# Sliding-window attention and a gated MLP on one core: queries permuted in blocks, the order restored in the output transposes

## The chip, the cores and the metric

The kernel runs on one core of a Trainium2 chip. The core has five engines with queues of their own: TensorE (PE, matmuls, with its weight loads shown as PEld), VectorE (DVE), ScalarE (ACT), GpSimd (POOL) and SyncE (SP). DMA is started from the queues of SyncE, ScalarE and GpSimd. The metric is the device time of one execution in microseconds, the median of several runs. A profile is one further execution, in which every instruction is recorded.

## The reference

Attention has 8 batches, 8 heads, 576 tokens and a head dimension of 64; all inputs are float32. Each query sees itself and the 127 tokens before it, and a bias grows with the distance, with another slope for each head. The result of all heads, 4608 tokens by 512, goes through an MLP with 2048 hidden units.

```
scores = scale * np.matmul(q, k.transpose(0, 1, 3, 2))
rel = pos[:, None] - pos[None, :]
mask = (rel >= 0) & (rel < window)
scores = np.where(mask, scores + bias[None], -1000000000.0)
attn = np.exp(scores - np.max(scores, axis=-1, keepdims=True))
attn = attn / (np.sum(attn, axis=-1, keepdims=True) + 1e-09)
attn_out = np.matmul(attn, v)
x = attn_out.transpose(0, 2, 1, 3).reshape(B * S, H * D)
h = x @ w_in
out = (h * (1.0 / (1.0 + np.exp(-beta * h)))) @ w_out
```

## The kernel before

**Attention of batches 0 and 1** works by pairs of heads, p = 0 to 3, on the first 512 tokens. get_pair loads q or k of a pair with four tokens in a row to each partition, so that a partition reads 1 KB at once; partition r holds tokens 4r to 4r+3. get loads v with the tokens of a block of 128 in the order c, r (token 4r+c on partition 32c+r), in four DMAs of 64 KB, one for each c. cast_pair and cast_v turn these to bf16 on GpSimd. TP transposes q and k on TensorE, and VectorE copies them into QK: k in blocks of 128 tokens, each in the order c, r, and q in the order c, r over all 512 tokens. SP_ computes scores with keys on the partitions. The first matmul puts the bias and the mask from a table into PSUM, the others add k times q. To get queries in their natural order, SP_ reads q with a stride: 128 elements lie between neighbours. A visit "A" covers three pieces (384 columns a head), "B" the other four (512 columns). "A" writes the PSUM tile SS and "B" the tile SX, two banks each. ScalarE's exp makes pt. PVP multiplies with v, and norm divides by the sum, which is a column of ones in VS. XP transposes the result by four matmuls with an identity and VectorE copies it into XT. The last 64 tokens of both batches are a tail: TT, SCT, PV and X, with the tables tablet.

**Batches 2 to 7** load whole blocks, transpose q and k by DMA (DT), and compute scores with SC, without tables: exp with a bias for each partition, and a multiplication by masks on VectorE.

**The MLP** works on groups g of 512 tokens. Hm or HS computes one of 16 hidden blocks, j, by four matmuls of 512 columns into a bank of psum_h, of which there are two; ScalarE's tanh and a VectorE operation write gT. OS multiplies with W2 into the tile ops. load_w1 and load_w2 are DMAs from GpSimd's queue that cast to bf16.

**Order.** TensorE, SyncE and GpSimd run in the written order throughout; ScalarE and VectorE do so in the first block (L574 to L626), and after it their order is a planner's. The first block is batch 0. On SyncE it issues p0, p1, p2, p3, v2, v3 (q and k of a pair, blocks of v) and beta; v0 and v1 are issued by ScalarE after constants. Then come batch 1's loads, and the first of them waits until w1[1] has landed:

```
g = get_pair("q", 1, 0)
after(g, w1[1])
```

On GpSimd, constants_late and the masks of batches 2 and up (constants_masks) precede the casts of batch 1. A DMA's issue can wait for an earlier DMA to land, and for the buffer of the fst pool (13 of them) to come free. The list second (L661) interleaves batch 1's attention with H of group 0, and spread places the steps of batches 2 and up (att) between the matmuls of the later groups: from item 22 of 40 on for group 1.

Of the kernel before, what the change touches and what calls it, by code (L numbers as in the profile page):

```python
# [19 lines left out]
def kernel(  # L20
# [39 lines left out]
    qtok = const.tile([P, P], F32, name="qtok")  # L60
    pen = const.tile([P, P], F32, name="pen")
    rel = const.tile([P, 3, P], F32, name="rel")
    relt = const.tile([P, 64], F32, name="relt")
    zeros = const.tile([P, 512], BF16, name="zeros")
    table = const.tile([P, H, 3, P], BF16, name="table")
    tablet = const.tile([P, 2, 2, NP, 64], BF16, name="tablet")
# [36 lines left out]

    def constants():
        nc.vector.memset(zeros[:], 0.0)
        nc.vector.memset(warm[:], 0.0)
        nc.scalar.activation(out=warm[:], in_=warm[:], func=ACTF.Exp)
        for _ in range(8):  # L110
            nc.tensor.matmul(
                SS[:, 0, :], lhsT=zeros[:, 0:P], rhs=zeros[:], start=True, stop=True,
                skip_group_check=True)
        for c in range(4):
            nc.gpsimd.iota(
                ktok[32 * c : 32 * c + 32], pattern=[[0, 1]], base=c, channel_multiplier=4,
                allow_small_or_imprecise_dtypes=True,
            )
        nc.gpsimd.iota(
            qtok[:], pattern=[[1, P]], base=0, channel_multiplier=0,  # L120
            allow_small_or_imprecise_dtypes=True,
        )
        make_identity(nc, ident[:])
        nc.vector.tensor_scalar(
            out=qtok[:], in0=qtok[:], scalar1=ktok[:, 0:1], scalar2=None, op0=ALU.subtract)
        for a, cmp in ((0, ALU.is_lt), (1, ALU.is_ge)):
            nc.vector.tensor_scalar(
                out=pen[:], in0=qtok[:], scalar1=0.0, scalar2=FAR, op0=cmp, op1=ALU.mult)
            nc.vector.scalar_tensor_tensor(
                out=rel[:, a], in0=qtok[:], scalar=float(P * a), in1=pen[:], op0=ALU.add,  # L130
                op1=ALU.add)
        nc.vector.tensor_copy(out=rel[:, 2], in_=rel[:, 0])
        for h in range(H):
            nc.vector.tensor_scalar_mul(table[:, h], rel[:], -slopes[h] / qscale)
        for i in range(2):
            nc.vector.memset(VS[i][:, :, :, D : D + 1], 1.0)

    def constants_late():
        nc.gpsimd.iota(
            relt[:], pattern=[[1, 64]], base=0, channel_multiplier=-1,  # L140
            allow_small_or_imprecise_dtypes=True,
        )
        nc.gpsimd.affine_select(
            out=relt[:], in_=relt[:], pattern=[[1, 64]], base=0, channel_multiplier=-1,
            compare_op=ALU.is_ge, fill=FAR,
        )
# [116 lines left out]
    def TP(b, p):  # L263
        src = staged.pop((b, "p", p))
        tps = psum_t.tile([P, 2, 4, P], BF16, name="tps", tag="t")
        for i in range(2):
            for c in range(4):
                nc.tensor.transpose(out=tps[:, i, c], in_=src[:, i, c], identity=ident[:])
        qk = QK[b % 2]
        nc.vector.tensor_copy(  # L270
            out=qk[:, 0, p, 0:FULL], in_=tps[:, 0].rearrange("d c r -> d (c r)"))
        nc.vector.tensor_copy(
            out=qk[:, 1, p, 0:FULL].rearrange("d (n c r) -> d c n r", n=4, c=4),
            in_=tps[:, 1].rearrange("d c (n r) -> d c n r", n=4))

    def TT(b):

# [14 lines left out]

    def SP_(b, vis, p):
        qk = QK[b % 2]
        sps = SS if vis == "A" else SX
        w = WIDTH[vis]
        for e in range(2):
            t = table[:, 2 * p + e]
# [8 lines left out]
        for kb, at, q0, n in VISIT[vis]:  # L307
            for e in range(2):
                if vis == "B" and n == 256:
                    o = sps[:, e, 0:P]  # L310
                    o = bass.AP(tensor=o.tensor, offset=o.offset,
                                ap=[list(o.ap[0]), [384, 2], [1, P]])
                else:
                    o = sps[:, e, at : at + n]
                nc.tensor.matmul(  # L315
                    o, lhsT=qk[64 * e : 64 * e + 64, 1, p, P * kb : P * kb + P],
                    rhs=qk[64 * e : 64 * e + 64, 0, p, 0:FULL].rearrange(
                        "d (c r) -> d r c", c=4)[:, q0 // 4 : (q0 + n) // 4, :],
                    start=False, stop=True, skip_group_check=True,
                )  # L320
        pt = pt_pool.tile([P, 2, 512], BF16, name="pt", tag="pt")
# [147 lines left out]
    def Hm(g, j, cs):  # L469
# [1 line left out]
            gts[g] = gt_pool.tile([P, NFF, TOKG], BF16, name="gT", tag="gT")  # L471
        c0 = (g * TOKG) % XTR
        if cs[0] == 0:
            hs[g, j] = psum_h.tile([P, TOKG], F32, name="hps", tag="hps")
        hps = hs[g, j]
        for c in cs:
            nc.tensor.matmul(  # L477
# [95 lines left out]
    with tc.manual_schedule(engines={ENG.PE, ENG.SP, ENG.Pool}):  # L573
        with tc.manual_schedule(engines={ENG.Activation, ENG.DVE}):  # L574
            for w in ("p0", "p1", "v0", "v1", "p2", "p3", "v2", "v3"):
                n = int(w[1])
                if w[0] == "p":
                    get_pair("q", 0, n)
                    get_pair("k", 0, n)
                elif n >= 2:  # L580
                    get("v", 0, n)
            nc.sync.dma_start(out=bflat[:], in_=moe_beta.rearrange("(j p) -> j p", p=P))
            constants()
            for n in range(2):
                get("v", 0, n, nc.scalar)
            w1 = []
            cast_pair(0, 0)
            TP(0, 0)
# [90 lines left out]
        opening.close()  # L679
        late["o"] = ctx.enter_context(  # L680
            tc.tile_pool(name="psum_o", bufs=2, space=bass.MemoryType.PSUM))
        work = tail(1)
        b2 = jobs(2)
        after_w2 = [True]
# [85 lines left out]
```

## Time and profile before

| | us |
|---|---|
| runs, median of 5 | 366.49 |
| lowest, highest | 364.74, 367.74 |
| profiled execution, its time | 363.82 |
| its span in the trace | 362.1 |
| PE busy | 336.3 |
| ACT busy | 206.8 |
| DVE busy | 199.4 |
| POOL busy | 107.5 |

A time in the profile is counted from the span's start. In the page, a row of digits gives the busy share of each fortieth of the span (9.05 us) in tenths; PEclk is the clock that was granted to TensorE. In a timeline, the columns are start, duration, engine, line, operation, output and inputs, count, and in brackets the engine's idle time before, with what ended it. "SPq" and "ACTq" are issues of DMA by SyncE and ScalarE. In groups, the columns after the shapes are total busy time, mean ns of one, and idle time before them. A table of windows gives, for each stretch, PE's busy time, the granted clock, the DMA share and GB/s.

### The profile page before, as it was taken

The page shows a single profiled execution, that of the slowest core. Times are in us where ns is not written, and L with a number is a line of the kernel's source. Part 1 is how long each engine was busy: PE and PEld are TensorE (multiplying, and loading weights), DVE is VectorE, ACT ScalarE, POOL GpSimd, SP SyncE. Part 2 cuts the span into 40 slices and gives each one's busy share as a digit, 9 for nine tenths or more (in the row PEclk, how much of TensorE's full clock was granted, in tenths as well). Part 3 has the DMA queues.
Part 4 walks back from the last instruction along what each step waited for, and adds up shares of the span by engine and source line. Part 5 has one row for each costly group of instructions (what it writes and reads, how often), then busy time and mean ns, then how long its engine had stood idle before and what let it go on. Part 6 is the DMA issues. An engine that isn't in the chain of part 4 may idle for free.

```text
span 362.1 us, 6353 instructions
## 1 busy us (share of the span) xinstructions
PE 336.3 (93%) x2365; PEld 155.6 (43%) x2365; DVE 199.4 (55%) x447; ACT 206.8 (57%) x392; POOL 107.5 (30%) x206
## 2 busy tenths in 40 slices
PE   7496899799799999989999999999999999999994
PEld 2133334344245444444444444444454445444441
DVE  6036557554367578456738764875487546624500
ACT  1242465454777589458746776676677755426511
POOL 4299733403634342333132414131200010010010
PEclk9589999999899999999999999999999999999999
DMA  7599999993999999891929792971100010020021
GB/s 237 111 141 252 208 174 202 216 179 87 241 207 240 241 196 232 186 230 50 208 90 191 153 217 90 189 164 55 60 1 31 31 58 29 3 87 2 29 86 61
DMA packets 136512, 49.45 MB, mean 137 GB/s; under 512 B 125840, under 2 KB 134048, under 8 KB 136480
## 3 DMA queue, kind: packets, MB, share of 16 engines
q1 hardware_dynamic: 127360, 35.41, 51.0%
q0 software_dynamic: 6944, 13.11, 14.4%
q10 hardware_dynamic: 2176, 0.52, 0.7%
q8 instruction: 18, 0.29, 0.4%
q14 instruction: 14, 0.11, 0.1%
HBM read 36.71 MB, written 9.44 MB: 127 GB/s over the span
## 4 chain that ended last, share of the span: by engine, by line
PE 80%; DVE 8%; ACT 6%; DMA 3%; issue 2%; SPq 1%; ACTq 0%
PE ops L500 33%; PE hps L477 30%; ACT pt L415 4%; PE SS L405 4%; DVE gT L485 3%; DVE pt L419 2%; DMA fst<-in_k_dram 2%; PE pv L444 2%; PE SX L315 2%; PE pv L440 2%; PE xt L455 2%; PE SS L315 1%; ACT sig L484 1%; PE pv L345 1%; PE SX L304 1%
## 5 line engine op out<-in xcount | busy, mean ns | idle before, releaser
L477 PE MATMUL hps<-XT,W 128*128 128x512 bf16 x576 | 145.0, 380 | 5.4 <-DVE gT L485 3.9
L500 PE MATMUL ops<-W,gT 128*128 128x512 bf16 x576 | 142.4, 381 | 0.0
L484 ACT ACTIVATE sig<-hps,beta_h 128x512 bf16<-128x512 f32 x144 | 98.7, 691 | 70.9 <-PE hps L477 65.4
L485 DVE SCALAR_TENSOR_TENSOR gT<-sig,hps 128x512 bf16<-128x512 bf16 x144 | 97.7, 684 | 69.9 <-ACT sig L484 69.3
L415 ACT ACTIVATE pt<-SS,bias 128x256 bf16<-128x256 f32 (+1 forms) x192 | 75.2, 478 | 14.5 <-PE SS L405 14.5
L477 PEld LDWEIGHTS <-W 128*128 128x128 bf16 x576 | 51.8, 98 | 63.3 <-issue 12.7
L500 PEld LDWEIGHTS <-gT 128*128 128x128 bf16 x576 | 52.1, 98 | 56.6 <-issue 1.8
L513 POOL DMA_DIRECT2D out_dram<-osb x34 | 18.5, 543 | 193.3 <-ACT osb L506 193.1
L419 DVE TENSOR_TENSOR pt<-pt,mask 128x1024 bf16<-128x1024 bf16 x48 | 36.4, 758 | 16.5 <-ACT pt L415 16.3
L506 ACT ACTIVATE osb<-ops 128x512 f32<-128x512 f32 x36 | 21.8, 605 | 39.1 <-PE ops L500 39.1
L245 POOL CAST vs<-fst 128x512 bf16<-128x512 f32 (+1 forms) x40 | 24.3, 623 | 26.6 <-DMA fst<-in_v_dram 25.2
L329 DVE RECIPROCAL zs<-pv 128x4 f32<-128x4 f32 (+1 forms) x80 | 13.9, 176 | 31.3 <-PE pv L444 18.1
L330 DVE TENSOR_TENSOR xn<-pv,zs 128x256 bf16<-128x256 f32 (+1 forms) x64 | 26.9, 421 | 1.7
L232 POOL CAST bst<-fst 128x512 bf16<-128x512 f32 (+1 forms) x32 | 19.8, 620 | 12.9 <-DMA fst<-in_q_dram 8.3
L405 PE MATMUL SS<-qkT 64*128 64x256 bf16 (+2 forms) x240 | 19.2, 254 | 2.8 <-ACT pt L415 2.6
L233 POOL CAST bst<-fst 128x512 bf16<-128x512 f32 (+1 forms) x32 | 20.0, 624 | 4.9 <-DMA fst<-in_k_dram 4.8
L444 PE MATMUL pv<-vs,pt 128*128 128x65 bf16 x240 | 20.6, 193 | 0.0
L461 DVE COPY XT<-xt 128x512 bf16<-128x512 bf16 (+1 forms) x32 | 12.3, 385 | 14.1 <-PE xt L455 13.8
L444 PEld LDWEIGHTS <-pt 128*128 128x128 bf16 x240 | 16.1, 97 | 6.7
L405 PEld LDWEIGHTS <-qkT 64*128 64x128 bf16 x240 | 8.2, 94 | 22.3 <-issue 21.6
L440 PE MATMUL pv<-vs,pt 128*128 128x65 bf16 x192 | 17.4, 193 | 0.0
L322 ACT ACTIVATE pt<-SS 128x768 bf16<-128x768 f32 x8 | 6.5, 811 | 18.4 <-DMA fst<-in_v_dram 12.4
(72 smaller groups left out, 171.0 us busy)
## 6 DMA issues: line engine op xcount, KB each, us to landing
out_dram<-osb POOLq DMA_DIRECT2D x34, 256.0 KB, 2.9
fst<-in_q_dram SPq DMA_DIRECT2D x32, 256.0 KB, 5.2
fst<-in_k_dram SPq DMA_DIRECT2D x32, 256.0 KB, 5.1
fst<-in_v_dram SPq DMA_DIRECT2D x24, 256.0 KB, 3.8
W<-in_moe_w_in_dram POOLq DMA_DIRECT2D x4, 512.0 KB, 7.3
W<-in_moe_w_out_dram POOLq DMA_DIRECT2D x4, 512.0 KB, 8.7
fst<-in_v_dram SPq DMA_DIRECT2D x24, 64.0 KB, 4.5
fst<-in_q_dram SPq DMA_DIRECT2D x8, 128.0 KB, 3.7
```

The source lines that it names most:

```text
L245: return nc.gpsimd.tensor_copy(out=VS[b % 2][0:rows, sb, :, 0:D], in_=fs.pop(("v", b, sb))[0:rows])
L330: nc.vector.tensor_tensor(out=xn, in0=pv[0:nq, :, 0:D], in1=zs[0:nq].broadcast_to([nq, 4, D]), op=ALU.mult)
L405: nc.tensor.matmul(o, lhsT=qk[64 * e : 64 * e + 64, 1, p, P * kb : P * kb + P], rhs=qk[64 * e : 64 * e + 64, 0, p, P * kb : P * kb + nq], ...
L415: nc.scalar.activation(out=pt[:, e, cols], in_=sps[:, e, cols], func=ACTF.Exp, scale=qscale, bias=bias[:, half, h : h + 1],)
L419: nc.vector.tensor_tensor(out=pt[:], in0=pt[:], in1=masks[m][:], op=ALU.mult)
L440: nc.tensor.matmul(pv[:, hl, 0 : D + 1], lhsT=weights(b, qb - 1, h, 1), rhs=vs[:, qb - 1, h, 0 : D + 1], start=True, stop=False,)
L444: nc.tensor.matmul(pv[:, hl, 0 : D + 1], lhsT=weights(b, qb, h, 0), rhs=vs[:, qb, h, 0 : D + 1], start=qb == 0, stop=True,)
L477: nc.tensor.matmul(hps[:], lhsT=W1[:, c, bass.ts(j, P)], rhs=XT[:, c, c0 : c0 + TOKG], start=(c == 0), stop=(c == NDM - 1),)
L484: nc.scalar.activation(out=sig[:], in_=hps[:], func=ACTF.Tanh, scale=beta_h[:, j : j + 1])
L485: nc.vector.scalar_tensor_tensor(out=gts[g][:, j, :], in0=sig[:], scalar=1.0, in1=hps[:], op0=ALU.add, op1=ALU.mult)
L500: nc.tensor.matmul(ops_, lhsT=gT[:, j, i * P : i * P + P], rhs=W2[:, j, :], start=(j == 0), stop=(j == NFF - 1),)
L506: nc.scalar.mul(osb[:], ops_, 0.5)
```

## The change

1. Queries of batches 0 and 1 are stored as keys are, in blocks of 128 tokens, each in the order c, r (TP). SP_ reads q without a stride, and queries of scores are in the order c, r. The constant qtok, from which the bias table is made, is counted in that order.
2. XP restores the order. Its four transposes with an identity become four matmuls with a permutation matrix, perm, that constants makes from an iota (nat) and an is_equal on VectorE. The PSUM tile is float32, since these aren't transposes.
3. The tail's second table has the keys in the order c, r and the queries in natural order. It was a copy of a part of table; now constants_late makes it by four iotas and four selects on 32 partitions each, and its multiplications cover both tables at once.
4. All of v of batch 0 is issued by SyncE, in the order p0, p1, v0, v1, p2, p3, v2, v3.
5. load_w1(0) is issued after cast_pair(0, 3), and constants_masks after the last cast of batches 0 and 1. betas comes before constants_late.
6. SX is used in batch 0 alone; batch 1's "B" uses SS too. SX's two banks then go to the pool of ops, and H of group 0 uses them for j = 1, 3, 5, 7, so that it has four banks up to j = 7. Three H blocks, not two, start before XP(0, 3), and the list second is spread over one j fewer.
7. The steps of batch 2 begin at item 17 of group 1, not 22.

```diff
-    relt = const.tile([P, 64], F32, name="relt")
+    relt = const.tile([P, 2, 64], F32, name="relt")
+    nat = const.tile([P, P], F32, name="nat")
+    perm = const.tile([P, P], BF16, name="perm")
...
         nc.gpsimd.iota(
-            qtok[:], pattern=[[1, P]], base=0, channel_multiplier=0,
+            qtok[:].rearrange("p (c r) -> p c r", c=4), pattern=[[1, 4], [4, 32]], base=0, channel_multiplier=0,
...
+        nc.gpsimd.iota(
+            nat[:], pattern=[[1, P]], base=0, channel_multiplier=0,
...
+        nc.vector.tensor_scalar(
+            out=perm[:], in0=nat[:], scalar1=ktok[:, 0:1], scalar2=None, op0=ALU.is_equal)
...
-        nc.gpsimd.tensor_copy(
-            out=tablet[:, :, 1], in_=table[:, :, 1, 0:64].rearrange("k (p e) t -> k e p t", e=2))
+        for c in range(4):
+            rows = slice(32 * c, 32 * c + 32)
+            nc.gpsimd.iota(
+                relt[rows, 1], pattern=[[1, 64]], base=P - c, channel_multiplier=-4,
...
+            nc.gpsimd.affine_select(
+                out=relt[rows, 1], in_=relt[rows, 1], pattern=[[-1, 64]], base=c - 1,
...
         for h in range(H):
             nc.gpsimd.tensor_scalar_mul(
-                tablet[:, h % 2, 0, h // 2], relt[:], -slopes[h] / qscale)
+                tablet[:, h % 2, :, h // 2], relt[:], -slopes[h] / qscale)
...
-        nc.vector.tensor_copy(
-            out=qk[:, 0, p, 0:FULL], in_=tps[:, 0].rearrange("d c r -> d (c r)"))
-        nc.vector.tensor_copy(
-            out=qk[:, 1, p, 0:FULL].rearrange("d (n c r) -> d c n r", n=4, c=4),
-            in_=tps[:, 1].rearrange("d c (n r) -> d c n r", n=4))
+        for i in range(2):
+            nc.vector.tensor_copy(
+                out=qk[:, i, p, 0:FULL].rearrange("d (n c r) -> d c n r", n=4, c=4),
+                in_=tps[:, i].rearrange("d c (n r) -> d c n r", n=4))
...
-        sps = SS if vis == "A" else SX
+        sps = SX if vis == "B" and b == 0 else SS
...
-                    rhs=qk[64 * e : 64 * e + 64, 0, p, 0:FULL].rearrange(
-                        "d (c r) -> d r c", c=4)[:, q0 // 4 : (q0 + n) // 4, :],
+                    rhs=qk[64 * e : 64 * e + 64, 0, p, q0 : q0 + n],
...
-        xt = psum_t.tile([P, 4, P], BF16, name="xt", tag="t")
+        xt = psum_t.tile([P, 4, P], F32, name="xtp", tag="t")
         for n in range(4):
-            nc.tensor.transpose(out=xt[:, n, :], in_=xn[:, n, :], identity=ident[:])
+            nc.tensor.matmul(xt[:, n, :], lhsT=xn[:, n, :], rhs=perm[:], start=True, stop=True)
...
-            hs[g, j] = psum_h.tile([P, TOKG], F32, name="hps", tag="hps")
+            if g == 0 and j < 8 and j % 2:
+                hs[g, j] = late["o"].tile([P, DM], F32, name="hpx", tag="ops")
+            else:
+                hs[g, j] = psum_h.tile([P, TOKG], F32, name="hps", tag="hps")
...
-                elif n >= 2:
+                else:
                     get("v", 0, n)
...
-            for n in range(2):
-                get("v", 0, n, nc.scalar)
...
-            w1.append(load_w1(0))
             TP(0, 2)
...
             cast_pair(0, 3)
+            w1.append(load_w1(0))
...
+            betas()
             constants_late()
-            betas()
-            for j in range(2):
+            opening.close()
+            late["o"] = ctx.enter_context(
+                tc.tile_pool(name="psum_o", bufs=2, space=bass.MemoryType.PSUM))
+            for j in range(3):
                 Hm(0, j, range(3))
             XP(0, 3)
-            for j in range(2):
+            for j in range(3):
                 Hm(0, j, range(3, 4))
...
-        constants_masks()
         cast_pair(1, 0)
...
             cast_v(b, 4)
+        constants_masks()
...
-        for j in range(2, NFF):
+        for j in range(3, NFF):
             HS(0, j)
-            to = len(second) * max(0, j + 1 - 4) // (NFF - 4)
+            to = len(second) * max(0, j + 1 - 5) // (NFF - 5)
...
-        spread([wrap(it, n) for n, it in enumerate(items)], 22, len(items) - 2, need[2])
+        spread([wrap(it, n) for n, it in enumerate(items)], 17, len(items) - 2, need[2])
```

More of the change, by code (lines that the diff above doesn't have):

```diff
@@ L123, in constants @@
         make_identity(nc, ident[:])
+        nc.gpsimd.iota(
+            nat[:], pattern=[[1, P]], base=0, channel_multiplier=0,
+            allow_small_or_imprecise_dtypes=True,
+        )
         nc.vector.tensor_scalar(
@@ L136, in constants @@
             nc.vector.memset(VS[i][:, :, :, D : D + 1], 1.0)
+        nc.vector.tensor_scalar(
+            out=perm[:], in0=nat[:], scalar1=ktok[:, 0:1], scalar2=None, op0=ALU.is_equal)
     def constants_late():
         nc.gpsimd.iota(
-            relt[:], pattern=[[1, 64]], base=0, channel_multiplier=-1,
+            relt[:, 0], pattern=[[1, 64]], base=0, channel_multiplier=-1,
             allow_small_or_imprecise_dtypes=True,
@@ L143, in constants_late @@
         nc.gpsimd.affine_select(
-            out=relt[:], in_=relt[:], pattern=[[1, 64]], base=0, channel_multiplier=-1,
+            out=relt[:, 0], in_=relt[:, 0], pattern=[[1, 64]], base=0, channel_multiplier=-1,
             compare_op=ALU.is_ge, fill=FAR,
         )
-        nc.gpsimd.tensor_copy(
-            out=tablet[:, :, 1], in_=table[:, :, 1, 0:64].rearrange("k (p e) t -> k e p t", e=2))
+        for c in range(4):
+            rows = slice(32 * c, 32 * c + 32)
+            nc.gpsimd.iota(
+                relt[rows, 1], pattern=[[1, 64]], base=P - c, channel_multiplier=-4,
+                allow_small_or_imprecise_dtypes=True,
+            )
+            nc.gpsimd.affine_select(
+                out=relt[rows, 1], in_=relt[rows, 1], pattern=[[-1, 64]], base=c - 1,
+                channel_multiplier=4, compare_op=ALU.is_ge, fill=FAR,
+            )
         for h in range(H):
             nc.gpsimd.tensor_scalar_mul(
-                tablet[:, h % 2, 0, h // 2], relt[:], -slopes[h] / qscale)
+                tablet[:, h % 2, :, h // 2], relt[:], -slopes[h] / qscale)
         for i in range(2):
@@ L676 @@
                 done += 1
-        opening.close()
-        late["o"] = ctx.enter_context(
-            tc.tile_pool(name="psum_o", bufs=2, space=bass.MemoryType.PSUM))
         work = tail(1)
```

## The prediction

> **What bounds the kernel now.** I read the page's row of slices first. TensorE is at nine tenths or more nearly everywhere, except in the first quarter; DMA is full from slice 3 to slice 9.
>
> ```profile
> PE   7496899799799999989999999999999999999994
> PEclk9589999999899999999999999999999999999999
> DMA  7599999993999999891929792971100010020021
> ```
>
> So from about 76 us on time is matmul work, which the diff leaves as it is; a gain must come from the first 100 us. Second, the timeline of the first 60 us, where batch 0 goes wrong:
>
> ```profile
> 4.87 7.44 SPq L207 DMA_DIRECT2D fst<-in_v_dram  x8
> 9.35 5.33 ACTq L207 DMA_DIRECT2D fst<-in_v_dram  x8
> 14.73 0.81 ACT L322 ACTIVATE pt<-SS 128x768 bf16<-128x768 f32 x1 [12.43 <-DMA fst<-in_v_dram]
> 22.68 1.03 PE L315 MATMUL SX<-qkT 64*128 64x128 bf16 x6
> 26.57 1.03 PE L315 MATMUL SX<-qkT 64*128 64x128 bf16 x6
> 27.63 0.38 SPq L223 DMA_DIRECT2D fst<-in_q_dram  x1
> 36.22 1.89 PE L477 MATMUL hps<-XT,W 128*128 128x512 bf16 x8 [1.28 <-DVE gT L485]
> 38.75 1.02 PE L477 MATMUL hps<-XT,W 128*128 128x512 bf16 x4 [0.64 <-DVE gT L485]
> 51.37 0.62 POOL L245 CAST vs<-fst 128x512 bf16<-128x512 f32 x1 [6.11 <-DMA fst<-in_v_dram]
> 54.43 0.41 PE L345 MATMUL pv<-vs,pt 128*128 128x65 bf16 x8
> ```
>
> The first scores are complete at 8.42 us (L315 starts at 7.61 and takes 0.81), but ScalarE issues eight v loads until 14.68 and the exp runs at 14.73: 6.3 us lost. Later, v of batch 1 is cast at 51.99 and its first user, the matmuls of PVP(1,"B",0), starts at 54.43: 2.4 us of slack. Third, groups with shapes apart, of the first 92 us and of the rest:
>
> ```profile
> L315 PE MATMUL SS<-qkT 64*128 64x256 bf16 x16 | 4.7, 589 | 2.4 <-DVE qkT L272 2.4
> L315 PE MATMUL SS<-qkT 64*128 64x128 bf16 x16 | 3.2, 392 | 0.0
> ```
>
> ```profile
> L405 PE MATMUL SS<-qkT 64*128 64x256 bf16 x144 | 16.5, 279 | 2.8 <-ACT pt L415 2.6
> L405 PE MATMUL SS<-qkT 64*128 64x64 bf16 x48 | 4.7, 189 | 0.0
> ```
>
> L315 reads q with 128 elements between neighbours: (589-392)/128 = 1.54 ns a column. L405 reads neighbours: (279-189)/192 = 0.47.
>
> **The change, part by part.**
>
> *Contiguous q.* Four L405 matmuls of 256 columns end in 0.39 us (timeline at 154.52); heads e = 0 and 1 run together, so that is 2 x 256 columns in a row. A "B" score group is also 512 columns a head, and takes 1.03: saving 0.64. An "A" group (384) takes 0.81 and should take some 0.34: saving 0.47. A pair saves 1.11 us, a batch 4.4. The q copy in TP takes the form of the k copy: 446 ns (L270) to 414 (L272), nothing.
>
> *v by SyncE.* ScalarE starts at 8.7, not 14.73. In batch 0, pair 3's cycle is 26.57-22.68 = 3.89; less 1.11, plus some for VectorE's two copies, which still stand between transposes and scores, it is 3.0. First SX group ends at 9.92 now; after, 9.92-1.11+0.28 (the perm mask on VectorE ahead of the first copy, at the price of L124, 128x128, 0.286) = 9.1. Three cycles: 18.1; with 0.5 for the clock (below) 18.6, against 27.60: **-9.0**. The Trainium skill ("DMA: Bandwidth & Descriptors", Issuing engines are not separate DMA queues) says issue from several engines saves only sequencer time, usually small. By that the move is worth eight issues, at the median 0.46 us each 3.7 us; the row says 6.3, because the issues also wait for earlier loads to land. I take the row: by the rule the early part would be -6.4, TensorE's own path below -10.0 instead of -12.6, and the end, set by DMA, the same.
>
> On SyncE v0 and v1 now stand ahead of p2, p3, and behind these v2, v3, beta and batch 1. Here too an issue waits for landings, not for its 0.4 us (SyncE's waits at L207: 5.4 us on q and 2.7 on k). So I cost bytes. From 2 to 10 us q/k moved 2.3 MB at 290 GB/s; v alone, 12 to 16, went at 150. Twelve tiles are 3 MB: 2.5 MB from about 2 us at 290 is 8.6, the last 0.5 at 150 is 3.3, gaps 1: all landed at 15, p3 at 12. Upper bound by the v issues' own row, 0.93 us each (7.44/8): 2.8+7.4+2.1+7.4 = 19.7, landing at the median 3.7 later, 23.4. I take 15 since the 0.93 were waits for tiles four times as large.
>
> *POOL.* load_w1(0) moves behind cast_pair(0,3), 0.9 us of issue. p3 is cast by 13, w1(0) issued by 14, v2 and v3 cast by 16.3, w1(1) issued then instead of at 21.23: -4.9; taking 0.5 off for W1 and v sharing DMA, **-4.4**. w1(1)'s landing opens batch 1's loads (27.63 now), so the whole DMA stream, full at 1.14 from 38 to 80, moves by 4.4. constants_late grows: eight more selects and iotas at 0.23 to 0.24 us, eight longer multiplies (0.37 each for 64 columns; +0.06 if as the selects at L165, at most double), less one 0.61 copy: +1.8 to +4.2, I take +2. The masks (3.9 us from 30.30) leave the place before cast_pair(1,0). Net -1.9, so this cast waits for its load alone. The masks now run behind cast_v(1,4), where POOL sat idle 3.67 before 63.75, and are not needed until batch 2's L419: nothing. Their 16 bias operations (0.14 each) go with them, off the end of batch 0 on VectorE.
>
> *perm in XP.* Matmul for transpose: same 128x128 form, 219 ns, nothing. The copy reads f32: between 0.42 (L357, bf16) and 0.68 (L485, f32 of 512 columns from PSUM); I take 0.68, as TENSOR_TENSOR of 256 f32 takes the same 0.42 as 512 bf16. +0.26 each; eight copies are 2.1 us, on the path only at XP(0,3) (+0.26), elsewhere covered by H matmuls; uncovered it would be +1 in batch 1.
>
> *Four H banks.* The waits at 36.22 and 38.75 go: **-1.9**. The two added banks are SX's, whose last exp is done before the first H matmul, as closing it early needs. Three H rows instead of two before XP(0,3), and betas ahead of constants_late, only reorder work.
>
> *One score tile in batch 1.* SX is given up. SP_(1,"A",1) directly follows SP_(1,"B",0) and now waits for its exp, 1.02 + 0.2; the others have an H group (0.87) and a transpose or PV between: **+1.3** (0.3 to 5, if tanh is queued ahead of each exp).
>
> *spread from item 17.* Four score groups follow each other closely at 93-102, where TensorE waits for ScalarE (1.57 us for a group's four exps, plus tanh). Begun at item 17, one item more lies between them, then fewer per item: **-1.0** (-3 to +1).
>
> **Clock.** The skill ("TensorE: Matmul & The Clock Gate", the HAM clock gate) has half clock follow an idle window of about 3.4 us. The trace is harsher:
>
> ```profile
> 94.00:95.00 1.00, 0.00 (x0) 1.00 1.05 312
> 95.00:96.00 1.00, 0.71 (x6) 0.85 1.29 278
> 96.00:97.00 1.00, 1.00 (x4) 0.50 1.34 220
> ```
>
> A gap of 1.91 us before 95.29 was enough. By the rule no gap that I foresee counts; by the row a wait for batch 1's v costs another 3.4 us window at half clock, up to 1.7 us of matmuls. I add **+0.5** there: 358.2 in place of 357.7 by the rule.
>
> **Sum.** TensorE alone would reach PVP(1,"B",0) at -9.0 -1.9 -3.3 (six groups) +1.3 +0.3 = -12.6, at 41.8. Its v arrives at 51.99-4.4 = 47.6 and is used at 47.7: -6.7. So most of the early gain turns into a wait for DMA. Then the last two groups -1.1, spread -1.0, clock +0.5: **-8.3**. The profiled execution takes 363.82 (span 362.1): 355.5. The runs' median 366.49 is 0.7% above it; with the same difference, **358.2**.
>
> **Rivals.**
>
> *TensorE's path counts in full*: DMA loses 6 us of idle around 10-20 (share 0.40) and batch 1's v comes with it. For: DMA stands still from 16 to 18. Against: full share from 20. -12.6 -1.1 -1.0 +1.0 (VectorE's added copies uncovered) = -13.7: 352.8.
>
> *Less*: loads of batch 0 land at 18 and the gate moves by only 1.5 us; 366.49 -1.5-2.4+0.1 -1.1 -1.0 +1.5 = 362.1.
>
> *Slower*: SyncE's queue. If each v issue takes 0.93 us or more, v(0,3) is cast at 24.7, w1(1) issued at 25.9, 4.7 late, v(1,3) is cast at 56.7: +2.4 over the slack, and the wait brings a half-clock window (+1.7), less 1.1 and 1.0: 368.5. It decides from w1(1) issued some 3 us late (at 24) on, 1 us for 1 us after that. Against: the bytes.
>
> *Nothing*: q's stride is not what makes L315 slow (the reads of two heads collide, say), and the gate moves little: 366. Against: L405 has the same 64 rows and two heads.
>
> **How the numbers follow.** Within 0.5% (1.8 us) is what a measurement of this kernel can't tell from no change. Forecast (356 to 361) 0.52; full path (under 356) 0.21; less (361 to 364.7) 0.12; same 0.06; slower 0.09. Faster is 0.85. The range 351.5 to 364.5 holds the forecast, nearly all of less and most of the full path, 0.82; the forecast's own is 356 to 361.
>
> **What would show it.** The first exp near 8.7; L315 groups 0.34 to 0.4; the last SX score group of batch 0 near 18.6; w1(1) issued near 16.3; no wait of hps on gT before j = 8; a wait of POOL for v(1,3) and of TensorE at PVP(1,"B",0) near 47.7; ScalarE released SS once for over 1 us. If w1(1) is issued after 21 us, or TensorE doesn't stand at PVP(1,"B",0), the sum is wrong.

## The result and the profile after

The kernel after takes 363.96 us (median of 28 runs, 359.42 to 369.63), the kernel before 367.00 (47 runs, 362.83 to 368.81). The ratio is 0.9901, with an interval of 0.9874 to 0.9927: faster by 1.0%, where the forecast of 358.2 asked for 2.3%. The ratio leaves out the runs that are more than 1.5% above the fastest of their kernel (10 of 28 after, 4 of 47 before), and so do the times given below, by which the kernel after takes 362.80; with all runs the medians' quotient is 0.9917. 363.96 lies in the predicted range near its upper end, and in the case called "less" (361 to 364.7), but not for the reason that this case gave.

The two profiled executions are not typical in the same way. That of before took 363.82, 3.2 below the median of its runs; that of after took 364.70 (span 362.8), 0.7 above its own. Profile against profile, the changed kernel is 0.9 slower; the ratio of the runs decides that it is faster. The profiles serve below to place the time.

The granted clock differs between executions of the same kernel. Of 81 runs of the kernel before beside the experiments, 45 with a mean clock of 0.960 or less took 366.3 to 368.7, and 22 with 0.969 to 0.981 took 363.0 to 365.7, but for one of 368.0; the other 14, four of them at 0.995, took 364.1 to 368.2. The profiled execution of before has 0.981, so the full clock that it shows below need not hold for the median run, and how much of the 1.0% is clock stays open.

The page's row of slices for the kernel after (one digit for each 9.07 us):

```profile
PE   6887856799799999989999999999999999999995
PEclk9889989799899999999999999999999999999998
DMA  7899999962999999993938793972100010010012
```

The second slice rose from 4 to 8: the early part became dense. But slices 6 and 7 (45 to 63 us), which were at 9 before, are now at 5 and 6, and in slices 6 to 8 (45 to 73 us) the granted clock, which was 9 there throughout, is at 8, 9 and 7. The timeline of the kernel after, in the same columns as before, shows both sides:

```profile
8.83 0.81 ACT L337 ACTIVATE pt<-SS 128x768 bf16<-128x768 f32 x1 [6.54 <-PE SS L331]
16.69 2.25 POOL L269 DMA_DIRECT2D W<-in_moe_w_in_dram  x3
18.80 0.40 PE L331 MATMUL SX<-qkT 64*128 64x128 bf16 x6
24.25 0.39 SPq L240 DMA_DIRECT2D fst<-in_q_dram  x1
37.59 0.48 PE L320 MATMUL SS<-table,ident 128*128 128x384 bf16 x2 [1.12 <-ACT pt L337]
45.15 0.33 PE L360 MATMUL pv<-vs,pt 128*128 128x65 bf16 x5
48.84 0.61 POOL L262 CAST vs<-fst 128x512 bf16<-128x512 f32 x1 [5.65 <-DMA fst<-in_v_dram]
49.51 0.25 PE L360 MATMUL pv<-vs,pt 128*128 128x65 bf16 x3 [4.03 <-POOL vs L262]
...
58.77 0.61 POOL L262 CAST vs<-fst 64x512 bf16<-64x512 f32 x1 [4.21 <-DMA fst<-in_v_dram]
59.34 0.14 POOL L193 IOTA kpos<- 128x1 f32 x1
59.51 1.06 DVE L206 TENSOR_SCALAR bias<-kpos 128x1 f32<-128x1 f32 x16 [1.15 <-POOL kpos L193]
60.49 0.68 DVE L372 CAST XT<-xtp 128x512 bf16<-128x512 f32 x1
61.23 0.27 PE L371 MATMUL xtp<-perm,xnp 128*128 128x128 bf16 x2 [2.44 <-DVE XT L372]
```

The first exp runs at 8.83 instead of 14.73 and the last SX scores of batch 0 end at 19.20 instead of 27.60: 8.4 us gained. At 45.48 TensorE has done five of the eight matmuls of PVP(1,"B",0) and stands until 49.51, since v(1,3) is cast only at 49.45. These matmuls end at 49.76 instead of 54.84, so 5.1 us are left. Then a second stop: the last cast_v of batch 1 waits 4.21 us for its load; behind it on GpSimd stands the iota for kpos; VectorE waits for kpos with 16 bias operations; behind them on VectorE stands the copy of XT that empties a PSUM tile; and TensorE waits 2.44 us for that tile. (The 0.88 at 62.38, for xnp, is no part of this: in e6, below, where the bias is early, the same matmuls wait 1.09.) The waits of TensorE (us in total, times, longest us), from 28 to 82 us:

```profile
PE pv L360 <- POOL vs L262: 4.0, 1, 4.0
PE xtp L371 <- DVE XT L372: 2.4, 1, 2.4
...
PE SS L320 <- ACT pt L337: 1.1, 1, 1.1
PE xtp L371 <- DVE xnp L345: 1.1, 2, 0.9
...
PE hps L495 <- DVE gT L503: 0.2, 1, 0.2
```

The windows of the kernel after (length, busy time of PE, PEld, DVE, ACT, POOL with counts, granted clock, DMA share, GB/s) show what follows such stops:

```profile
48.00:52.00 4.00, 2.49 (x17) 0.94 (x16) 1.01 (x3) 0.73 (x2) 3.13 (x5) 0.78 1.29 202
52.00:56.00 4.00, 3.69 (x43) 2.23 (x42) 2.71 (x8) 2.02 (x3) 1.91 (x4) 0.79 1.25 184
...
60.00:64.00 4.00, 1.90 (x17) 0.91 (x17) 3.08 (x16) 0.44 (x1) 4.00 (x15) 0.99 0.87 187
64.00:68.00 4.00, 3.75 (x38) 1.77 (x36) 1.30 (x4) 1.96 (x3) 2.67 (x5) 0.58 1.03 210
68.00:72.00 4.00, 2.39 (x11) 1.05 (x12) 1.66 (x5) 0.66 (x1) 1.23 (x2) 0.84 1.06 209
72.00:76.00 4.00, 4.00 (x21) 1.52 (x19) 2.11 (x4) 1.67 (x4) 0.00 (x0) 0.73 1.18 239
```

In the profile of the kernel before, all of these stretches had a clock of 1.00; two of them:

```profile
48.00:52.00 4.00, 4.00 (x33) 1.43 (x30) 2.60 (x6) 2.33 (x4) 0.63 (x2) 1.00 1.25 205
64.00:68.00 4.00, 2.88 (x42) 1.59 (x43) 2.13 (x5) 2.14 (x3) 2.21 (x4) 1.00 1.18 226
```

In the kernel after, three stretches of about 3.4 us at half clock lie between 50 and 74 us (from about 50.3, 63.9 and 70.8). From 40 to 76 us the mean clock is 0.86, where it was 1.00. 0.14 of 36 us is 5.0: so much matmul time at most went there, and less where TensorE stood anyway.

The first matmul of the output (L518) starts at 77.28; in the kernel before (L500) at 76.54. From there to the end of the span it is 285.52 us after and 285.56 before. So **the whole difference arises ahead of the first output matmul**, and by then this execution has given back the 5.1 us and 0.7 more. The wait for XT (2.4) and the clock (up to 5.0) have room for these 5.8. In all sixteen kernels profiled here, this remainder is between 285.0 and 286.1 us, so the start of the first output matmul serves below as the measure of a profile.

### The profile page after: what moved, and what is told of

Its sections match the earlier page's. It is cut to its first block, busy times and chain, and to the rows that moved or that the text cites. A ratio compares the mean times of both kernels' runs of the same rounds, so it can differ in the third digit from the quotient of the medians.

```text
span 362.8 us, 6367 instructions
## 1 busy us (share of the span) xinstructions
PE 333.6 (92%) x2365; PEld 157.1 (43%) x2365; DVE 203.0 (56%) x448; ACT 206.4 (57%) x392; POOL 109.3 (30%) x214
## 2 busy tenths in 40 slices
DMA packets 136511, 49.45 MB, mean 136 GB/s; under 512 B 125840, under 2 KB 134048, under 8 KB 136480
## 4 chain that ended last, share of the span: by engine, by line
PE 70%; DMA 11%; DVE 6%; ACT 5%; POOL 3%; issue 2%; SPq 1%; POOLq 0%; ACTq 0%
PE ops L518 32%; PE hps L495 28%; DMA fst<-in_v_dram 7%; PE SS L420 4%; ACT pt L430 3%; DMA fst<-in_k_dram 3%; DVE pt L434 3%; DVE gT L503 2%; PE pv L459 2%; PE pv L455 2%; PE xt L470 2%; DMA fst<-in_q_dram 1%; ACT sig L502 1%; POOL tablet L167 1%; POOL vs L262 1%
## 5 line engine op out<-in xcount | busy, mean ns | idle before, releaser
L518 PE MATMUL ops<-W,gT 128*128 128x512 bf16 x576 | 141.9, 380 | 0.0
L502 ACT ACTIVATE sig<-hps,beta_h 128x512 bf16<-128x512 f32 x140 | 96.0, 691 | 80.5 <-PE hps L495 75.0
L503 DVE SCALAR_TENSOR_TENSOR gT<-sig,hps 128x512 bf16<-128x512 bf16 x140 | 94.9, 683 | 62.3 <-ACT sig L502 61.5
L518 PEld LDWEIGHTS <-gT 128*128 128x128 bf16 x576 | 52.3, 98 | 57.2 <-issue 2.0
L434 DVE TENSOR_TENSOR pt<-pt,mask 128x1024 bf16<-128x1024 bf16 x48 | 37.9, 791 | 16.4 <-ACT pt L430 16.1
L337 ACT ACTIVATE pt<-SS 128x768 bf16<-128x768 f32 (+1 forms) x12 | 10.6, 881 | 14.9 <-PE SS L331 14.8
```

The source lines that it names most:

```text
L434: nc.vector.tensor_tensor(out=pt[:], in0=pt[:], in1=masks[m][:], op=ALU.mult)
L502: nc.scalar.activation(out=sig[:], in_=hps[:], func=ACTF.Tanh, scale=beta_h[:, j : j + 1])
L503: nc.vector.scalar_tensor_tensor(out=gts[g][:, j, :], in0=sig[:], scalar=1.0, in1=hps[:], op0=ALU.add, op1=ALU.mult)
L518: nc.tensor.matmul(ops_, lhsT=gT[:, j, i * P : i * P + P], rhs=W2[:, j, :], start=(j == 0), stop=(j == NFF - 1),)
```

## The experiments

My theory after reading the trace: TensorE's path is as short as the sum said, and the time was lost to two late loads (v(1,3) directly, v(1,4) by way of kpos) and to the half clock behind their waits. A rival: the path itself gained less than the sum, so that taking the waits away gives little. A second rival, for the first wait: loads that start earlier bring v earlier. A kernel's ratio is always to the kernel before, run beside it; the medians of the latter were between 366.53 and 367.47.

**Parts alone.** e1_contig is the kernel before with items 1 to 3 of the change only (contiguous queries, perm, the tail's table):

```diff
-                    rhs=qk[64 * e : 64 * e + 64, 0, p, 0:FULL].rearrange(
-                        "d (c r) -> d r c", c=4)[:, q0 // 4 : (q0 + n) // 4, :],
+                    rhs=qk[64 * e : 64 * e + 64, 0, p, q0 : q0 + n],
...
-            nc.tensor.transpose(out=xt[:, n, :], in_=xn[:, n, :], identity=ident[:])
+            nc.tensor.matmul(xt[:, n, :], lhsT=xn[:, n, :], rhs=perm[:], start=True, stop=True)
```

> The kernel before with parts 1 to 3 of the change alone (contiguous q, permutation matrix in XP, second tail table); v0 and v1 still issued by ScalarE, masks early, two H banks, SX kept, spread from 22. Theory A (the matmuls get shorter by 4.4 us in batch 1, but v of batch 1 arrives as before, at 52, with 2.4 us of slack, so that a gain beyond 2.4 up to PVP(1,B,0) turns into a wait): L331 groups of 0.34 and 0.40, TensorE waits for v(1,3) some 1 to 2 us, time -3 us. Rival B (TensorE's own path is all that counts): -6 us or more and no wait for v. Rival C (the f32 copies and the permutation cost what the matmuls save): 0.

Measured: 364.02, ratio 0.9928 (0.9895 to 0.9960). e2_vsp is the kernel before with v by SyncE only:

```diff
-                elif n >= 2:
+                else:
                     get("v", 0, n)
...
-            for n in range(2):
-                get("v", 0, n, nc.scalar)
```

> The kernel before with v of batch 0 issued by SyncE in the new order, nothing else. Theory A: first exp near 8.9 instead of 14.73; the cycle of a pair stays 3.9, so the last SX scores of batch 0 end near 9.9 + 3 x 3.9 = 21.6 instead of 27.6; w1(1) issued near 17 to 19; v(1,3) cast 2 to 3 us earlier than 52, which is what the end gains with the slack of 2.4: -3 to -4 us. Rival B (early time counts in full): -6. Rival D (SyncE's queue becomes the limit): v(1,3) no earlier than 52, time 0 or slower.

Measured: 363.17, ratio 0.9915 (0.9880 to 0.9950). Each part alone gives 0.7 to 0.85%, and the whole change gives 1.0%: the parts seem not to add, though their intervals nearly allow it. Neither shows a wait for v(1,3) in its profile: PVP(1,"B",0) starts at 53.79 in e1 and 53.76 in e2, late enough for v. So in e1 the median came as expected, but not by the wait for v that was expected with it. Its longest wait of TensorE between 28 and 78 us:

```profile
PE bps L177 <- POOL identf masks.py:199: 4.2, 1, 4.2
```

There betas stands behind the longer constants_late on GpSimd. The change puts betas first, and this wait isn't in its profile; so the reordering that I called "only reorder work" may be worth something with the longer constants_late. It wasn't run apart. In e2 the first exp is at 8.46, but the clock is at half from 10.0 to 33.9 us; how much of the gain this took away wasn't measured.

**The bias operations.** e3_bias is the kernel after with the iota of kpos in constants_late, and the bias loop ahead of cast_pair(1, 0); the masks stay late:

```diff
...
+    def biases():
         for h in range(H):
             for half in range(2):
...
+        biases()
         cast_pair(1, 0)
...
```

> The changed kernel with the iota kpos in constants_late and the 16 bias operations of VectorE made before batch 1's casts; the masks stay late. Theory A (in the changed kernel these operations stand in VectorE's order ahead of a copy that frees a PSUM tile, wait for kpos behind the cast of v(1,4), and stop TensorE 2.4 + 0.9 us, and a half-clock window follows): both waits go, -3 to -5 us against the changed kernel, that is -6.5 to -8 against the kernel before. Rival E (TensorE would wait for the tail's loads, q, k and v of the last 64 tokens, at the same place anyway): the wait moves to TT or PV of the tail and less than 1 us is won.

Measured: 362.09, ratio 0.9892 (0.9841 to 0.9943); 0.7 below the kernel after where 3 to 5 were expected, and with overlapping intervals. In its profile the wait for XT is down to 0.24 and the first output matmul is at 74.62 instead of 77.28. But there v(1,4) is cast at 54.62, not 59.38, so that kpos need not have been late anyway (in e8, below, it stays behind v(1,4), cast at 54.72, and VectorE doesn't wait for it). And the wait for v(1,3) is now 5.02 us long, with half clock from 46.3 to 53.1. Alone, this didn't settle it.

**More DMA, earlier.** e4_gate opens batch 1's loads one weight block sooner:

```diff
-                after(g, w1[1])
+                after(g, w1[0])
```

> The changed kernel with batch 1's first load gated by the landing of w1[0], not w1[1]. Theory A (batch 1's loads are late because of the gate, and v(1,3) stops TensorE for 4.0 us): batch 1's loads start near 21 instead of 24.25, v(1,3) is cast 2 to 3 us earlier, the wait shrinks by as much, -1 to -3 us against the changed kernel. Rival F (DMA is full, so that an earlier start only shares the same bandwidth with W1): v(1,3) moves by less than 1 us and H waits for W1 instead; 0.

Measured: 363.20, ratio 0.9929 (0.9891 to 0.9967), no gain (0.4 above the kernel after). The first load of batch 1 is issued at 21.09 instead of 24.25, but its timeline has v(1,3) later than in the kernel after:

```profile
50.87 0.61 POOL L262 CAST vs<-fst 128x512 bf16<-128x512 f32 x1 [7.30 <-DMA fst<-in_v_dram]
51.54 0.32 PE L360 MATMUL pv<-vs,pt 128*128 128x65 bf16 x3 [5.68 <-POOL vs L262]
```

So in this stretch, with DMA full, an earlier start isn't an earlier arrival, and the second rival falls; this is one profile, of an execution of 365.94, but the median gained nothing either. The next run changes what shares the DMA engines with v.

**The order of the weights.** e6_order is e3_bias with the weights issued near their use: block 2 of W1 after cast_pair(1, 1), block 3 after cast_pair(1, 3), all of W2 after cast_v(1, 3):

```diff
-            w1 += [load_w1(n) for n in range(1, 4)]
+            w1.append(load_w1(1))
...
+        w1.append(load_w1(2))
...
-        w2 = [load_w2(0), load_w2(1)]
...
+        w1.append(load_w1(3))
...
-        w2 += [load_w2(2), load_w2(3)]
+        w2 = [load_w2(n) for n in range(4)]
```

> The changed kernel with the early bias of the third run, and DMA in another order: W1's third and fourth parts are issued behind batch 1's first casts, and all of W2 behind the cast of v(1,3). Theory A (what holds TensorE at PVP(1,B,0) is v(1,3) behind 3 MB of weights that nobody needs yet): v(1,3) is cast near 42 to 44 instead of 49.4, the wait of 4 to 5 us goes, so does the half-clock stretch behind it, -3 to -6 us against the third run (362.1), about 357. Rival F (all of the early DMA is needed in any order, so that the wait only moves to W1 in H or to W2 in the first output blocks): H waits for W1(2) or W1(3), first output matmul not before 74, time 361 to 363.

Measured: 355.88, ratio 0.9725 (0.9667 to 0.9784), 6.9 below the kernel after and 6.2 below e3. The timeline of e6:

```profile
42.23 1.17 POOL L264 CAST vs<-fst 128x512 bf16<-128x512 f32 x2
43.34 2.97 POOL L275 DMA_DIRECT2D W<-in_moe_w_out_dram  x4
44.63 0.42 PE L362 MATMUL pv<-vs,pt 128*128 128x65 bf16 x8
```

v(1,3) is cast at 43.40, six us sooner than in the kernel after, and PVP(1,"B",0) runs through at 44.63. The first output matmul is at 68.56. The first rival falls as far as it says that taking the waits away gives little. But 44.63 is not the 41.8 at which the sum has TensorE here: its path is some 3 us longer than my theory said.

Is it the order of the weights, or the order together with the bias? Two runs answer. e11_order_before makes the same edit to the weights in the kernel before, and nothing else:

> The kernel before with only its weights' DMA in the other order (W1's last two parts behind batch 1's first casts, W2 behind the cast of v(1,3)). Theory A (DMA's order limits only a kernel whose first part is faster; here v(1,3) has 2.4 us of slack): v(1,3) is cast several us before 52, nothing waits for it, 0 to -1 us. Rival G (the order of the weights is worth its 6 us whatever else is changed, by less crowding of DMA): -4 us or more.

Measured: 367.34, ratio 1.0008 (0.9979 to 1.0037): nothing, as expected. v(1,3) is cast at 46.57, but TensorE comes for it only at 58.53. (That is later than the 54.43 of the kernel before: this profile, of an execution of 368.15, has half clock from about 30 to 37 and 40 to 43 us, where that of the kernel before has the full one.) e14_order_alone makes it to the kernel after, so that it is e6 without the edit of e3 (here against e6; the iota goes back too):

```diff
...
-        biases()
         cast_pair(1, 0)
...
```

> The changed kernel with the weights' DMA in the new order alone; the masks, kpos and the 16 bias operations stay late. If VectorE's wait for kpos is a cost of its own: v(1,4) is cast near 60 to 62 here, TensorE reaches the same copy near 51, so the wait grows to 8 us or more and most of the gain of the new order is lost: 361 to 364. If the wait is hidden behind other work: as with the early bias, 356.

Measured: 367.97, ratio 1.0026 (0.9984 to 1.0067). I expected 361 to 364: all of the gain is lost, and the order that gives 6.2 us with the bias loop early costs 5.2 with it late. Its timeline:

```profile
62.95 0.61 POOL L262 CAST vs<-fst 64x512 bf16<-64x512 f32 x1 [2.72 <-DMA fst<-in_v_dram]
63.69 1.06 DVE L206 TENSOR_SCALAR bias<-kpos 128x1 f32<-128x1 f32 x16 [7.02 <-POOL kpos L193]
65.41 0.37 PE L371 MATMUL xtp<-perm,xnp 128*128 128x128 bf16 x2 [8.32 <-DVE XT L372]
```

The same matmuls in e6:

```profile
53.63 0.27 PE L373 MATMUL xtp<-perm,xnp 128*128 128x128 bf16 x2 [0.23 <-DVE XT L374]
```

v(1,3) is in time (46.23), TensorE runs ahead, and the weights that now come between v(1,3) and v(1,4) make the latter late (63.56 instead of 59.38). VectorE stands 7.02 us and TensorE 8.32 for 16 operations of a column each. That is 8.1 of the 12.1 us between e14 and e6; in e14's profile TensorE also comes to PVP(1,"B",0) 3.7 later (48.32), behind 1.74 for W1 and half clock from about 43 to 46, and the clock is at half again from 60.0 to 70.2. So the two waits stand in series, and the first covers part of the second: with the one for v away, the one for kpos grows from 2.44 to 8.32. (The 5.02 for v in e3 is not the reverse: that wait comes first, v(1,3) is cast at 49.41 as in the kernel after, and TensorE only came 1.0 sooner.) Together the two edits are worth 6.9 us.

**Four H banks and one score tile.** e8_sx keeps SX in batch 1 and two H banks, with two H rows before XP(0, 3), in the kernel after; e12_order_sx does so in e6:

```diff
-        sps = SX if vis == "B" and b == 0 else SS
+        sps = SS if vis == "A" else SX
...
-            if g == 0 and j < 8 and j % 2:
-                hs[g, j] = late["o"].tile([P, DM], F32, name="hpx", tag="ops")
-            else:
-                hs[g, j] = psum_h.tile([P, TOKG], F32, name="hps", tag="hps")
+            hs[g, j] = psum_h.tile([P, TOKG], F32, name="hps", tag="hps")
...
-            for j in range(3):
+            for j in range(2):
```

> The changed kernel with SX kept for batch 1 and two H banks, two H blocks before XP(0,3). Prediction's terms: H banks -1.9, one score tile +1.3; undone, +0.6. Theory A (both are ahead of PVP(1,B,0), which waits for v(1,3) anyway): no difference in time, the wait of 4 us at PVP(1,B,0) shrinks or grows instead. Rival B (TensorE's path counts): +0.6.

> The kernel of the run with the weights behind v (355.9) with SX kept in batch 1, two H banks and two H blocks before XP(0,3). Now that TensorE's path sets the time, the prediction's terms should be seen: +1.9 for the banks, -1.3 for the score tile, +0.6 together. If the banks are worth nothing since batch 1's first pair lands at 29 and holds TP(1,0) anyway: -1.3.

Measured: e8 359.26, ratio 0.9831 (0.9759 to 0.9903), 3.5 below the kernel after, where no difference or 0.6 above was expected; e12 354.31, ratio 0.9642 (0.9605 to 0.9678), 1.6 below e6, near the 1.3 expected if the banks are worth nothing. Both pairs of intervals just overlap, but both profiles agree: the first output matmul is at 74.36 instead of 77.28, and at 66.79 instead of 68.56. In e8's, though, v(1,4) is cast at 54.72 instead of 59.38 and the wait for kpos is missing, so that its gain need not be item 6's; e12 against e6 is the cleaner pair. TensorE's waits from 28 to 92 us, first in e6, then in e12:

```profile
PE xtp L373 <- DVE xnp L347: 1.3, 2, 1.1
PE hps L497 <- DMA W<-in_moe_w_in_dram: 1.3, 1, 1.3
PE SS L333 <- DVE qkT L290: 1.1, 1, 1.1
PE SS L322 <- ACT pt L339: 1.1, 1, 1.1
...
PE hps L497 <- DVE gT L505: 0.2, 1, 0.2
```

```profile
PE hps L494 <- DVE gT L502: 1.6, 2, 1.3
...
PE xtp L373 <- DVE xnp L347: 0.5, 1, 0.5
PE SS L333 <- DVE qkT L290: 0.2, 1, 0.2
```

With two banks, the waits of H for gT come back (0.2 to 1.6); with the second score tile, the wait for pt goes (1.1), those for xnp and qkT shrink (2.4 to 0.7), and in the same kernel no wait for W1 remains (1.3). So item 6 seems to take away more than it gives here. The two halves of it weren't run apart, so which of these follows from the tile and which from the number of H rows stays open.

**The spread.** e7_spread22, e10_order22 and e15_best put the 22 back, in the kernel after, in e6 and in e12:

```diff
-        spread([wrap(it, n) for n, it in enumerate(items)], 17, len(items) - 2, need[2])
+        spread([wrap(it, n) for n, it in enumerate(items)], 22, len(items) - 2, need[2])
```

> The changed kernel with the steps of batch 2 from item 22 again. By the prediction's term this loses 1.0 us. By the traces so far the stretch from the first output matmul to the 97th takes 45.0 us in the changed kernel and 44.4 in the one before, so that the term has the wrong sign: 0 to -1 us against the changed kernel.

> The kernel of the run with the weights behind v (355.9) with the steps of batch 2 from item 22. In four traces with 17 the stretch from the first to the fourth output tile of group 0 and 1 takes 26.4 to 27.0 us, in four with 22 it takes 25.7 to 25.9: -0.7 against 355.9, that is 355.2. By the prediction's term: +1.0.

> The kernel of the run with the weights behind v and SX kept (354.3), with the steps of batch 2 from item 22: -0.7 as between the two kernels before it, 353.6.

Measured: 361.91 (ratio 0.9884, 0.9840 to 0.9929), 355.20 (0.9668, 0.9626 to 0.9709) and 354.50 (0.9639, 0.9615 to 0.9664): 0.9 and 0.7 below their counterparts, and for e15 0.2 above, where 0.7 below was expected; all inside the intervals. From the first output matmul to the end of the span it is 285.03, 284.97 and 285.05 with 22, and 285.52, 285.54 and 285.21 with 17. Starting sooner gains nothing; it costs 0.2 to 0.6 there.

**The stride, on a path that is not covered.** e13_order_strided is e6 with the strided read of q, the transposes with an identity and the bf16 copy:

```diff
-                    rhs=qk[64 * e : 64 * e + 64, 0, p, q0 : q0 + n],
+                    rhs=qk[64 * e : 64 * e + 64, 0, p, 0:FULL].rearrange(
+                        "d (c r) -> d r c", c=4)[:, q0 // 4 : (q0 + n) // 4, :],
```

> The kernel of the run with the weights behind v (355.9) with the strided q, the identity transposes and the bf16 copy of the kernel before. The matmuls' term of the prediction is 1.11 us a pair: +4.4 in batch 1 and up to +3.3 in batch 0 if TensorE's path sets the time, less some 0.3 for the f32 copy: +4 to +7 against 355.9, that is 360 to 363. If loads still hold batch 1 in this kernel: +1 to +2.

Measured: 365.14, ratio 0.9972 (0.9932 to 1.0013): 9.3 above e6, more than expected, where the same items alone gave 3 in e1. The matmuls' own time explains 1.11 x 8 = 8.9 at most, less what the f32 copy costs. The rest is seen in the windows; two stretches of e13, then the same two of e6:

```profile
24.00:28.00 4.00, 3.06 (x34) 2.32 (x34) 3.40 (x22) 0.14 (x1) 3.64 (x8) 0.50 0.42 132
28.00:32.00 4.00, 4.00 (x13) 1.51 (x11) 0.84 (x7) 0.00 (x0) 2.43 (x6) 0.50 0.97 235
```

```profile
24.00:28.00 4.00, 3.10 (x17) 1.53 (x17) 1.60 (x12) 0.58 (x1) 3.76 (x8) 1.00 0.50 152
28.00:32.00 4.00, 3.34 (x22) 1.52 (x19) 3.81 (x7) 3.23 (x6) 3.88 (x9) 1.00 1.04 241
```

e13 runs 8 us at half clock where e6 has the full one; this is one profile of each.

**The clock by itself.** e9_keep is e3 with 16 matmuls of 512 columns, whose result nobody reads, ahead of PVP(1,"B",0), so that TensorE is busy while it waits:

```diff
-            lambda: PVP(1, "B", 0), lambda: (SP_(1, "A", 3), PVP(1, "A", 2)),
+            lambda: (busy(16), PVP(1, "B", 0)), lambda: (SP_(1, "A", 3), PVP(1, "A", 2)),
```

> The third run's kernel (early bias) with 16 added matmuls of 512 columns, whose result nobody reads, just ahead of PVP(1,B,0): 3.5 us at full clock, inside the wait of 4 to 5 us. If half clock after the wait is a cost of its own, the windows at half clock after 46 go and the time falls by 1 to 2 us against the third run (362.1); if the clock costs nothing because DMA sets the pace on to the end of that stretch, 0; if the matmuls delay the path, +1 to +3.

Measured: 360.53, ratio 0.9868 (0.9806 to 0.9929), against 0.9892 (0.9841 to 0.9943) of e3. The 1.6 below e3 is what was expected, but the run is inconclusive: the intervals overlap, v(1,3) came at 52.0 in its profile (of an execution of 364.37), so that TensorE still waited 2.7 us behind the added work, and half clock still followed (0.50 from 54 to 56 us). What the half clock alone costs is not settled.

The best kernel, e12, takes 354.31, 3.6% less than the kernel before and 2.3% less than the kernel after; e15, the same with the 22, can't be told from it.

## Why the prediction was only half right

| step | predicted | the profile after |
|---|---|---|
| first exp | 8.7 | 8.83 |
| L331 groups, "A" and "B" | 0.34, 0.40 | 0.34, 0.40 |
| last SX scores of batch 0 | 18.6 | 18.80 to 19.20 |
| w1(1) issued | 16.3 | 16.69 |
| v(1,3) cast | 47.6 | 49.45 |
| TensorE reaches PVP(1,"B",0) | 41.8 | 45.15 |
| TensorE at PVP(1,"B",0) | stands until 47.7 | stands until 49.51 |
| ScalarE's hold of SS | +1.3 | +1.12 |
| waits of H for gT before j = 8 | gone | 0.20 left |
| late masks and bias | 0 | a wait of 2.44 |
| clock | +0.5 | half clock for three stretches from 50 to 74 |
| spread | -1.0 | 0 (0.2 to 0.6 worse) |

**Contiguous q** was right in size and cause. The groups by form of the kernel after, to 92 us:

```profile
L331 PE MATMUL SS<-qkT 64*128 64x256 bf16 x24 | 3.6, 295 | 4.7 <-DVE qkT L288 4.7
L331 PE MATMUL SS<-qkT 64*128 64x128 bf16 x32 | 3.5, 230 | 0.0
```

(295-230)/128 = 0.51 ns a column, where the stride took 1.54. The step from L405's read of neighbours to these groups held, so the rival "nothing" falls. **v by SyncE** was right too: 8.4 us of the 9.0, and SyncE's queue made no one late, so the rival "slower" did not come. Here the row (6.3 us of held exp) was a better guide than the rule weighed against it, that of the Trainium skill ("DMA: Bandwidth & Descriptors", Issuing engines are not separate DMA queues), by which the move saves eight issues, 3.7 us.

**The gate** was the first mis-sized term. w1(1) was issued 4.5 sooner (4.4 in the sum), but the first load of batch 1 only 3.4 sooner, since W1 took longer to land (8.5 us at the median instead of 7.3), and v(1,3) only 2.5 sooner, not 4.4. The step "the whole DMA stream moves by 4.4" took the stream as rigid. It shares the engines with whatever else is issued (e4: a gate 3.2 sooner, v 2.0 later; e6: less weight ahead, v 6.0 sooner). That TensorE would stand at this point was said rightly.

**TensorE's own path** was mis-sized too: 9.3 us shorter at PVP(1,"B",0), not 12.6. From the last SX scores of batch 0 to this point the sum takes 3.6 off the 26.83 us of the kernel before, which leaves 23.2; the kernel after takes 25.95. Half clock from 22.8 to 26.4 accounts for 1.8 of these 2.7 us at most (mean clock 0.93), and two waits for VectorE grew by 1.1, those for qkT (1.13 instead of 0.26) and for XT at the first H blocks (0.78 instead of 0.52). In e6, at full clock, the stretch takes 25.8, with the same two waits and 1.29 for W1. The wait for v hid this in the kernel after.

**The masks** are the step that failed. "Not needed until batch 2's L419: nothing" looked at the consumer of the data and not at the queue in which the small operations stand. I named the work queued behind constants_masks on GpSimd, and that there was idle time for it. I didn't ask what stands behind the 16 bias operations on VectorE: in the planner's order it is the copy of XT. So one late load, v(1,4), which nothing else needed soon, stopped GpSimd, VectorE and TensorE in turn: for TensorE 2.44 us instead of the predicted nothing in the kernel after, and 8.32 in e14 against 0.23 in e6, where only the bias differs.

At the first output matmul the sum had -6.7 -1.1 +0.5 = -7.3, the profile has +0.7. Of the 8.0 between them, v's lateness is 1.8 (49.51 instead of 47.7) and the wait for XT 2.4; the rest, 3.8, is no more than the 5.0 that the clock can account for, but was not measured apart.

**The clock term** was too small. I allowed for one stretch behind one wait; from 40 to 76 us there were three. By the rule ("TensorE: Matmul & The Clock Gate", the HAM clock gate: an idle window of some 3.4 us) at most the stop of 4.03 us counts, by the row (a gap of 1.91 us is enough) that of 2.44 too. The profile after is harsher than both: the stretch from 70.8 came behind stops of at most 1.17 us since 63.9, and one from 22.8 to 26.4, which I hadn't foreseen at all, behind stops of at most 0.53 since 17.8. So a list of the long stops would not have given the number of stretches.

**Banks, score tile, spread.** The waits at 36.22 and 38.75 went and that for pt came, both as predicted. But the -1.9 was counted as if a removed wait were a gain to the end; TensorE was on its way to a wait for v there. Keeping SX gives back 1.6 in e12. The -1.0 of the spread has no support in any of the three pairs.

Of the rivals, *TensorE's path counts in full* (352.8) is not reached: with both waits out of the way it is 355.9, and with SX kept 354.3, which is no longer the change that was predicted.

## What to carry to other kernels

Before a small operation is moved behind a late load, follow it through every in-order queue: what its producer stands behind, and what stands behind its consumer on the other engine; here 16 operations that take 1.06 us stopped TensorE for 2.4 to 8.3 us. Once a stretch is full of DMA, a gain ahead of it turns into a wait unless the loads are put in the order of their first use; issuing more of them earlier can make the needed one later. Of two waits in series the first hides part of the second, so an edit that undoes one of them alone may show little, or the wrong sign.

## What was not expected of the hardware

The clock fell to half behind stops of 2.4 to 4.0 us for about 3.4 us at a time, and in the kernel after also from 22.8 to 26.4, with TensorE recorded as busy for 3.50 of the 4.80 us before it; also in stretches where TensorE was recorded as busy for 2.4 to 3.75 of 4 us (64 to 72 us in the kernel after). In e13 it was 0.50 from 24 to 32 us with TensorE recorded as busy for 3.06 and 4.00 of each 4 us, so a busy record is no sign of full clock. The last point is the price of sharing: opening batch 1's loads 3.2 us sooner brought v(1,3) 2.0 us later (49.45 to 51.48), with a DMA share of 1.11 to 1.29 from 44 to 52 us in the kernel after. That is one pair of profiles, too little for a rule.
